# A third nested mixing product in layer two of a two-layer attention and gMLP kernel

## The chip, the cores and the metric

One core of one Trainium2 chip runs one launch of the kernel. TensorE (PE) multiplies, VectorE (DVE) and ScalarE (ACT) do elementwise work, GpSimd (POOL) does a little of that and issues some DMAs, SyncE (SP) issues most DMAs. The metric is the device time in microseconds. Three runs of the kernel before gave 1369.42 (median), 1368.47 and 1369.64.

## The reference

Everything is float32, S = 2048 tokens, D = 512, hidden half width 896. The kernel computes two layers, each an attention block and a mixer block with their own residuals; both layers use the same weights:

```python
def _A_ref(x, wqkv, wo):            # linear attention, 32 heads of 16
    q, k, v = ...                   # x @ wqkv
    phi = lambda t: jnp.where(t > 0, t + 1, jnp.exp(t)) + 1e-6
    kv = einsum("bhsd,bhse->bhde", phi(k), v); z = phi(k) summed over tokens
    ...                             # phi(q) kv / (phi(q) z + 1e-6), heads joined, @ wo

def _B_ref(x, w_in, w_sp, b_sp, w_out):
    z = _gelu(x @ w_in); z1 = z[..., :Fh]; z2 = _layernorm(z[..., Fh:])
    g = einsum("ts,bsf->btf", w_sp, z2) + b_sp[None, :, None]
    return (z1 * g) @ w_out

x = x + _A_ref(_layernorm(x), wqkv, wo)
x = x + _B_ref(_layernorm(x), w_in, w_sp, b_sp, w_out)
x = x + _A_ref(_layernorm(x), wqkv, wo)
x = x + _B_ref(_layernorm(x), w_in, w_sp, b_sp, w_out)
```

## The kernel before

**Number format.** A float32 operand is split into a rounded high part, made by ACT (`high`, L105), and a low part, value minus high, made by DVE (`low`, L108). A product is three matmuls: high by high, high by low, low by high (`mm3`, L119 to L121, and `acc`, L1389 to L1391).

**Stages of a layer.** P1 is the first attention phase over 16 token tiles: project K and Q, form phi, and accumulate the product of the tokens with phi(K). Then a transition, P2 (second attention phase and the mixer's first projection with gelu), a tail, P4 (the token mixing with `w_sp`, 2048 by 2048, then the gates and the output projection, called OUT below). Layer one's OUT also prepares layer two: `Make` (L173) builds kept sums of a weight, and `join` (L1611 on) loads and splits K's and Q's weights and starts the first tiles.

**One step of P1** (`P1.run`). Step s turns token tile s (DVE transpose L296, high L105 on ACT, `T_low` with L108 on DVE), projects K and, up to step 10, Q of tile s - 1 on TensorE, makes phi of each (ACT L363 and L364, DVE L365), splits the normalised tokens (L105, L108) and phi(K) (ACT L376, DVE L377), adds phi(K) to a running sum on POOL (L382), and multiplies tile s - 2 into the accumulators. TensorE's step has 36 matmuls in steps 3 to 10 and 24 in step 2 and from step 11 to step 16, since the last six Q products are put off. `ln_a` (statistics on DVE L230 and L232, three one-column operations on POOL L234, L235, L239) and `ln_b` (normalise on ACT, L245, and a store to be turned) run two steps ahead. From step 5 on pieces of later weights are split at the step's end (`piece`: a high on ACT, a low on DVE), one in step 5, then two until none is left.

**The mixing** (class `P4`). A Strassen-like scheme in seven block products over halves of tokens. P4, P1, P6, P7, P5 and P3 are its products; P1 and P2 of the top level can each be done by seven products of a second level ("nested", N1 and N2, operand halves from halves of token tiles). The order is a tuple of names, one for each layer:

```python
ORDERS = ("P4", "P1", "P6", "P7", "P5", "P3", "N2"), ("P4", "P6", "P7", "N1", "N2", "P5", "P3")
```

P4 and P5 have 8 steps of 24 matmuls, P6, P7 and P3 8 of 18, a nested product 14 of 12. Step g prepares the weight's split of step g + 2 and the token operand of step g + 3 (`prepare`, L1231 on: L1244 and L1253 for the weight, L1228 among the operands' sums, L1257 for their low), multiplies (`mm`, `nested_mm`), fetches the weight of step g + 4. After a product `evac` (L1427, L1448 for P5) or the end of `nested_mm` adds the banks into the gate units. A nested product needs sums of the mixing weight's blocks; class `Inner` makes them (`unit`, `finish`): load, add in place, high, low, two stores to DRAM, 16 kept pairs for each product. Layer two's N1 makes them in P2 and in the mixing's steps `MIX_UNITS`; N2's are left from layer one.

**Gates.** `gates` (L1404 on) multiplies a finished unit by the loaded z1 on POOL (L1411), with a subtraction ahead of it for some (L1409).

**OUT** (second loop of `P4.run`, and `o`). Step i: load the residual two tiles ahead, up to two gates, 21 matmuls of the output projection, the residual's add from the bank (L1514 on DVE), store, then `zsplit(i + 2)`: high of the gates' tile on ACT, low on DVE (L108, 896 columns). In layer one `Make.step` follows (four half sums, L186 to L189, then two highs and lows), and `late_adds` (L1472) at the start.

**What sets the order.** There is no scheduler: each engine runs its instructions in the program's order, and waits on semaphores that a framework places by use of tiles. Tiles come from hand-kept free lists (`pages` of 128x512, `quads`, `banks`), so a tile taken again waits for its last reader.

Of the kernel before, what the change touches and what calls it, by code (L numbers as in the profile page):

```python
# [15 lines left out]
P = 128  # L16
# [13 lines left out]
MIX_UNITS = (11, 15, 18, 20, 25, 31, 36, 40), (7, 9, 11, 13, 15, 17, 19, 21)  # L30
# [3 lines left out]
class Slots:  # L34
# [16 lines left out]
    def put(self, *tiles):  # L51
        for t in tiles:
            n, _ = self.held.pop(id(t))
            self.free_list.append(n)


@with_exitstack
def mixer_kernel(ctx: ExitStack, tc: tile.TileContext, x_in, wqkv, wo_d, win1_d, win2_d, wsp_d, bsp_d, wout_d,
# [114 lines left out]
    class Make:  # L173


        def __init__(self):
            self.raw, self.sum, self.part = {}, {}, {}

        def fetch(self, g):
            self.raw[g] = load(win1_d[g]), load(win1_d[g + 3])  # L180

        def add(self, g):
            a, b = self.raw.pop(g)
            A11, A12, A21, A22 = (r.rearrange("p (c f) -> p c f", f=P)[:, s] for r in (a, b) for s in (slice(0, 2), slice(2, 4)))
            s, t = pages.get([P, 2, 2, P]), pages.get([P, 2, 2, P])
            nc.vector.tensor_add(s[:, 0], A21, A22)  # L186
            nc.vector.tensor_sub(s[:, 1], s[:, 0], A11)
            nc.vector.tensor_sub(t[:, 0], A11, A21)
            nc.vector.tensor_sub(t[:, 1], A12, s[:, 1])  # L189
            pages.put(a, b)  # L190
            self.sum[g] = s, t

        def split(self, g):
            self.part[g] = []
            for r in self.sum.pop(g):
                h, l = pages.get([P, 2, 2, P], F32R), pages.get([P, 2, 2, P], F32R)
                split(h, l, r)
                pages.put(r)
                self.part[g] += [h, l]

        def store(self, g):
            for n, p in enumerate(self.part.pop(g)):
                m = 2 * (n // 2)
                nc.sync.dma_start(kept[:, m:m + 2, g, n % 2, :], p.bitcast(F32).rearrange("p m c f -> p m (c f)"))
                pages.put(p)

        def step(self, i):
            for g in range(3):
                at = i - 2 * g
                if 0 <= at < 5:  # L210
                    (self.fetch, lambda g: None, self.add, self.split, self.store)[at](g)
# [89 lines left out]
    class P1:  # L301
        def __init__(self, L):
# [8 lines left out]
            self.zacc = None  # L311

        def loadx(self, i):
            if i < NT:
                self.x[i] = load(xs[self.st, i])

        def ln_a(self, i):
            if i < NT:
                self.ms[i] = stats(self.x[i], 1, self.L + i == 0)

        def ln_b(self, i):
            if i >= NT:
# [173 lines left out]
        def run(self):  # L496
# [3 lines left out]
            self.wv = quads.get([P, 4, 512])  # L500
            ND = NT - DEFER
            for s in range(1, NT + 2):
                self.loadx(s + 3)
# [19 lines left out]
                if s <= NT:  # L523
                    self.xsplit(s - 1)
                    self.K_split(s - 1)
                if s + 1 < NT and s + 1 in self.turn.by_pe:
# [8 lines left out]
                if s <= 4:  # L535
                    c = s - 1
                    nc.sync.dma_start(self.wv[:, c, :], wqkv[c * P:(c + 1) * P, 1024:1536])
                else:
                    for _ in range(min(len(side), 1 if s < 6 else 2)):
                        side.popleft().piece()  # L540
                if s >= 4:
                    for w in list(side)[:1 if s < 5 else 2]:
# [73 lines left out]
    class P2:  # L616
# [200 lines left out]
        def fetch_sum(self, m):  # L817
            self.S[m] = []
            for g in range(3):
                t = pages.get([P, 2, 2, P], F32R)  # L820
                nc.gpsimd.dma_start(t.rearrange("p i c f -> p i (c f)"), kept[:, m - 1, g])
# [85 lines left out]
        def side(self, s):  # L907
# [7 lines left out]
            elif s == 17:  # L915
# [3 lines left out]
                self.fetch_sum(2)  # L919
            elif s == 18:  # L920
# [3 lines left out]
                self.fetch_sum(3)  # L924

        def run(self, sums):
            w1 = self.win1
            own = inner["N1" if self.seven else "N2"]
            for s in range(1, NT + 3):
# [28 lines left out]
                else:  # L958
# [19 lines left out]
                    if s <= NT + 1:  # L978
                        if not sooner:
                            self.d_high(s - 2)  # L980
                        if 6 <= s < 13 if self.seven else 14 <= s < 18:
# [18 lines left out]
                if self.seven:  # L1000
# [3 lines left out]
                    elif s in (8, 11):  # L1004
                        own.unit()
# [65 lines left out]
    class Inner:  # L1071
# [3 lines left out]
        def __init__(self, base):  # L1075
            self.base = base
            self.d = {m: dram.tile([2, P, 2, 2, 512], F32, name=f"n{base}_{m}") for m in range(1, 5)}
# [4 lines left out]
            self.free = None  # L1082

        def part(self):
            if self.free is None:
                return pages.get(PAGE, F32R)
# [4 lines left out]
        def fetch(self):  # L1091

            if self.ahead:
                k, u = self.ahead.popleft()
                b = self.base
                at = (((3, b), (3, b + 4)), ((2, b),), (), ((2, b + 4),))[u]
                for name, (n, s) in zip(("21", "22") if u == 0 else ("11",) if u == 1 else ("12",), at):
                    self.raw[name] = load(wsp_d[n, s + k])

        def out(self):  # L1100
            for m, k, n, p in self.parts:
                nc.sync.dma_start(self.d[m][k // 2][:, k % 2, n, :], p.bitcast(F32))
                if id(p) in pages.held:
                    pages.put(p)
            self.parts = []

        def finish(self, late=False):
# [7 lines left out]
            if not keep:  # L1115
                pages.put(t)
            self.parts = [(m, k, n, p) for n, p in enumerate((h, l))]
# [31 lines left out]

        def begin(self, n, ahead=2):  # L1150
# [6 lines left out]
    class P4:  # L1157
# [4 lines left out]
        ORDERS = ("P4", "P1", "P6", "P7", "P5", "P3", "N2"), ("P4", "P6", "P7", "N1", "N2", "P5", "P3")  # L1162
# [3 lines left out]
        NEST = ("P1", "P2", "P6", "P5", "P7", "P3", "P4")  # L1166
        OWN = {"P1": (2, 0), "P2": (2, 4), "P4": (3, 4)}
        SUM = {"P3": 4, "P5": 1, "P6": 2, "P7": 3}

        def __init__(self, p2, sums):  # L1170
# [11 lines left out]
            self.wout = {}  # L1182
            self.wraw = deque()
            self.wsteps = (48, 50, 51, 53, 55, 56, 57) if self.nest_late else range(60, 67)
            self.wloads = (45, 47, 48, 50, 52, 53, 54) if self.nest_late else range(60, 67)

        def fetch(self, g):
# [3 lines left out]
            if p[0] == "N" and self.NEST[k // 2] in self.SUM:  # L1191
# [483 lines left out]
```

## Time and profile before

| | |
|---|---|
| median of 3 runs | 1369.42 us (1368.47 to 1369.64) |
| span of the profiled execution | 1367.4 us, 18070 instructions |
| PE / DVE / ACT / POOL busy | 1361.1 / 990.2 / 618.1 / 462.5 us |
| DMA | 287.02 MB, mean 210 GB/s |
| PE stages of layer two, start | OUT of layer one 615.1, P1 691.2, transition 808.2, P2 823.6, tail 1002.9, P4 1026.0, P6 1069.5, P7 1102.2, N1 1134.8, N2 1172.9, P5 1211.0, P3 1254.5, OUT 1287.1 |

The span runs from the profile's first to its last event; the timed runs contain some time around it. A row of a timeline gives an instruction's start and duration, engine and line, output and inputs by tile name, and in brackets how long its engine was idle before and what it waited for. Matmuls overlap, so a matmul's shown duration isn't its share of the time; the distance between starts is. In the page's busy times PEld is the weight load, which lies beside PE.

### The profile page before, as it was taken

The numbers are of one execution on the slowest core, as the hardware profiler recorded it, in microseconds if no ns is written. First come the engines' busy times: TensorE is split into PE (matmuls) and PEld (weight loads), VectorE is DVE, ScalarE is ACT, GpSimd is POOL, SyncE is SP. The second block draws the span as 40 slices with busy tenths as digits, with TensorE's granted clock in tenths as the row PEclk, the third lists the DMA queues.
The fourth block names the chain that finished last, engine by engine and source line by source line (L and its number), as shares of the span: only waits on it lengthen the run. The fifth ranks groups of instructions, "written<-read, shape, count | busy, mean of one in ns | idle before, by whom it ended". The sixth has DMA issues, their size and how long they took to land.

```text
span 1367.4 us, 18070 instructions
## 1 busy us (share of the span) xinstructions
PE 1361.1 (100%) x6129; PEld 1141.0 (83%) x6129; DVE 990.2 (72%) x1471; ACT 618.1 (45%) x978; POOL 462.5 (34%) x537
## 2 busy tenths in 40 slices
PE   9999999999999999999999999999999999999998
PEld 7888888888888888888888888888888888888887
DVE  6775888765757789887667758887767578985742
ACT  6675544444443443441356655534454452442410
POOL 3333475433334137524123434543220001133350
PEclk9999999999999999999999999999999999999999
DMA  5542377877788988897944414777366569854452
GB/s 171 177 131 63 116 246 257 263 247 270 256 249 282 309 277 275 267 355 228 314 124 158 138 56 132 227 224 250 115 198 195 176 225 323 308 183 162 171 189 90
DMA packets 168957, 287.02 MB, mean 210 GB/s; under 512 B 14624, under 2 KB 58528, under 8 KB 165792
## 3 DMA queue, kind: packets, MB, share of 16 engines
q1 hardware_dynamic: 161808, 254.27, 57.7%
q0 software_dynamic: 5184, 28.31, 5.7%
q10 hardware_dynamic: 1872, 3.28, 0.6%
q8 instruction: 48, 0.79, 0.2%
q14 instruction: 45, 0.37, 0.1%
HBM read 196.94 MB, written 88.87 MB: 209 GB/s over the span
## 4 chain that ended last, share of the span: by engine, by line
PE 100%; DVE 0%; DVEq 0%; issue 0%
PE bank L121 19%; PE bank L120 19%; PE bank L119 19%; PE bank L1389 10%; PE bank L1390 10%; PE bank L1391 10%; PE bank L1329 3%; PE bank L1332 3%; PE bank L1331 3%; PE bank L840 1%; PE bank L841 1%; PE bank L839 1%; PE bank L257 1%; PE bank L580 1%; PE bank L445 0%; PE bank L476 0%
## 5 line engine op out<-in xcount | busy, mean ns | idle before, releaser
L1389 PE MATMUL bank<-qd,pg 128*128 128x512 f32 x608 | 236.5, 389 | 0.0
L1390 PE MATMUL bank<-qd,pg 128*128 128x512 f32 x608 | 236.5, 389 | 0.0
L1391 PE MATMUL bank<-qd,pg 128*128 128x512 f32 x608 | 236.5, 389 | 0.0
L1253 DVE TENSOR_TENSOR qd<-qd,qd 128x1024 fp32r<-128x1024 f32 x106 | 145.6, 1373 | 79.0 <-ACT qd L1244 78.4
L1244 ACT ACTIVATE qd<-qd 128x1024 fp32r<-128x1024 f32 x106 | 112.1, 1058 | 128.1 <-DVE qd L1253 52.6
L105 ACT ACTIVATE pg<-pg 128x512 fp32r<-128x512 f32 (+1 forms) x141 | 87.0, 620 | 165.7 <-DVE pg L296 49.4
L121 PE MATMUL bank<-qd,pg 128*128 128x512 f32 x380 | 148.4, 391 | 0.0
L234 POOL TENSOR_SCALAR rs<-mv 128x1 f32<-128x1 f32 x95 | 40.8, 430 | 305.1 <-DVE mv L232 304.7
L1050 POOL TENSOR_TENSOR pg<-pg,pg 128x512 f32<-128x512 f32 x64 | 95.9, 1499 | 135.8 <-DMA pg<-in_wsp_dram 106.4
L1391 PEld LDWEIGHTS bank<-qd,pg 128*128 128x128 f32 x608 | 114.1, 188 | 23.9
L1389 PEld LDWEIGHTS bank<-qd,pg 128*128 128x128 f32 x608 | 114.1, 188 | 23.7
L1390 PEld LDWEIGHTS bank<-qd,pg 128*128 128x128 f32 x608 | 114.1, 188 | 23.5
L1411 POOL TENSOR_TENSOR bg<-bg,pg 128x512 f32<-128x512 f32 x56 | 89.3, 1606 | 127.3 <-DMA pg<-z 123.0
L245 ACT ACTIVATE pg<-pg,nb,rs 128x512 f32<-128x512 f32 x63 | 51.1, 812 | 143.1 <-POOL nb L239 127.6
L119 PE MATMUL bank<-qd,pg 128*128 128x512 f32 x284 | 110.7, 390 | 0.0
L120 PE MATMUL bank<-qd,pg 128*128 128x512 f32 x284 | 110.6, 389 | 0.0
L108 DVE TENSOR_TENSOR pg<-pg,pg 128x512 fp32r<-128x512 f32 (+1 forms) x139 | 102.5, 739 | 11.1 <-DMA z<-pg 3.7
L119 PE MATMUL bank<-bg,qd 128*128 128x448 f32 x256 | 94.0, 367 | 0.0
L120 PE MATMUL bank<-bg,qd 128*128 128x448 f32 x256 | 93.6, 366 | 0.0
L121 PE MATMUL bank<-bg,qd 128*128 128x448 f32 x256 | 93.4, 365 | 0.0
L296 DVE STREAM_TRANSPOSE pg<-pg 128x512 f32<-128x512 f32 x79 | 85.4, 1081 | 9.9 <-DMA pg<-xt 3.4
L119 PE MATMUL bank<-wo,qd 128*128 128x512 f32 x224 | 87.1, 389 | 0.0
(192 smaller groups left out, 3053.9 us busy)
## 6 DMA issues: line engine op xcount, KB each, us to landing
qd<-s SPq DMA_DIRECT2D x64, 512.0 KB, 4.0
pg<-in_wsp_dram SPq DMA_DIRECT2D x96, 256.0 KB, 4.6
qd<-n POOLq DMA_DIRECT2D x24, 1024.0 KB, 7.9
qd<-in_wsp_dram SPq DMA_DIRECT2D x42, 512.0 KB, 4.4
s<-pg SPq DMA_DIRECT2D x64, 256.0 KB, 4.2
pg<-x SPq DMA_DIRECT2D x64, 256.0 KB, 3.6
n<-pg SPq DMA_DIRECT2D x60, 256.0 KB, 4.2
pg<-z SPq DMA_DIRECT2D x56, 256.0 KB, 4.1
```

The source lines that it names most:

```text
L105: nc.scalar.activation(h, src, AF.Copy)
L108: nc.vector.tensor_sub(l, src, h.bitcast(F32))
L119: nc.tensor.matmul(out, ah, bh, start=start, stop=False)
L120: nc.tensor.matmul(out, ah, bl, start=False, stop=False)
L121: nc.tensor.matmul(out, al, bh, start=False, stop=stop)
L1050: nc.gpsimd.tensor_tensor(t, a, b, op=OP.add)
L1244: nc.scalar.activation(wh, r, AF.Copy)
L1253: nc.vector.tensor_sub(wl, r, wh.bitcast(F32))
L1389: m(out, h[:, o], w[:, 0, j, :], start=start, stop=False, skip_group_check=True)
L1390: m(out, h[:, o], w[:, 1, j, :], start=False, stop=False, skip_group_check=True)
L1391: m(out, l[:, o], w[:, 0, j, :], start=False, stop=stop, skip_group_check=True)
L1411: nc.gpsimd.tensor_tensor(u, u, z1, op=OP.mult)
```

## The change

Layer two's product P4 is done as a third nested product, N4, at the end of the mixing.

- The order becomes P6, P7, N1, N2, P5, P3, N4. N4 runs its seven inner products as P1, P6, P2, P5, P7, P4, P3, and adds its banks straight into gate units that are filled by then (two operations each; six units get a copy on ACT during N2, steps 6 to 11). P5's eight steps each get two more DVE operations that prepare N4's operands (`fourth_operand`). P6's operand takes one add more. The gates of layer two move: eight single ones in P5, none in P3, six in N4, fourteen in OUT.
- N4's 16 kept pairs are made by a new method `staged`, one pipeline stage in each step: store the last pair, low of the one before (DVE), high of the one before that (ACT), add of the next (DVE), load ahead. Two adds lie in the last two steps of layer one's OUT, ten in P1's steps 1 to 10 of layer two (their lows up to step 12), four in the mixing's steps 47, 49, 51, 53. In P1 `staged` stands behind `K_split`, ahead of phi(Q), and takes its tiles from two quads cut in pages (`Views`). N1's pairs use `staged` too, in P2's steps from 6 on and the mixing's steps 1, 3, ..., 15.
- Layer two's first normalisation moves from P1 to layer one's OUT: statistics of tile i behind its residual add, `norm(i - 1)` on ACT at step i, a turned store; P1 then loads the normalised tile twice, once as it is and once turned. `ln_a` and `ln_b` do nothing in layer two.
- Pieces of later weights in layer two's P1: one in each of steps 5 to 15. V's weight is loaded in step 15.
- `Make` sums in place, at steps 1, 3 and 5, and splits one half in a step (2 to 7).
- Layer two's output weight is split earlier, in P5, P3 and N4, and OUT takes tokens 8 to 15 first.

Counted by engine, PE's rows go from 6014 to 5990, DVE's from 1440 to 1510, ACT's from 991 to 1017, POOL's from 542 to 544, SP's from 865 to 903.

```diff
-MIX_UNITS = (11, 15, 18, 20, 25, 31, 36, 40), (7, 9, 11, 13, 15, 17, 19, 21)
+MIX_UNITS = (11, 15, 18, 20, 25, 31, 36, 40), (1, 3, 5, 7, 9, 11, 13, 15)
+MAKE_AT = 0, 2, 4
+INNER_UNITS = range(47, 55, 2)
...
@@ P1 @@
+        def norm(self, i):
+            if i < 0:
+                return
+            x, y = self.x.pop(i), pages.get(PAGE)
+            normalise(feats(y, True), feats(x, False), self.ms.pop(i))
+            pages.put(x)
+            self.y = y
...
@@ P1.run @@
             for s in range(1, NT + 2):
+                if s == 2 and own is not None:
+                    self.send(NT - 1)
+                self.loadx(s + 3 if own is None else s + 1)
...
                     self.K_split(s - 1)
+                if own is not None and s <= NT:
+                    own.staged()
+                    if s == 1:
+                        self.norm(NT - 1)
...
@@ Inner @@
+        def staged(self, more=True):
+            self.out()
+            if self.open is not None:
+                m, k, h, t, keep = self.open
+                l = self.part() if keep else t
+                low(l if keep else t.bitcast(F32R), t, h)
...
+            if self.added is not None:
+                m, k, t, keep = self.added
+                h = self.part()
+                high(h if h.dtype == F32R else h.bitcast(F32R), t)
...
+            k, u = self.todo.popleft()
+            op = nc.vector.tensor_tensor
+            if u == 0:
+                self.S1 = t = self.raw.pop("22")
+                op(t, self.raw["21"], t, op=OP.add)
...
-        ORDERS = ("P4", "P1", "P6", "P7", "P5", "P3", "N2"), ("P4", "P6", "P7", "N1", "N2", "P5", "P3")
+        ORDERS = ("P4", "P1", "P6", "P7", "P5", "P3", "N2"), ("P6", "P7", "N1", "N2", "P5", "P3", "N4")
+        NEST["N4"] = "P1", "P6", "P2", "P5", "P7", "P4", "P3"
...
+        def fourth_operand(self, k):
+            a, b = ztile[k], ztile[k + HT]
+            nc.vector.tensor_sub(a[:, self.H1], a[:, self.H2], b[:, self.H1])
+            nc.vector.tensor_sub(a[:, self.H3], b[:, self.H3], a[:, self.H3])
...
@@ P4.nested_mm @@
+            if p == "N4":
+                for n, out in {"P1": ((1, self.X),), "P6": ((2, self.X),), "P2": ((1, self.Y),), "P5": ((4, self.Y),),
+                               "P7": ((4, self.X),), "P3": ((2, self.Y),), "P4": ((3, self.X),)}[name]:
+                    for i in range(2):
+                        f = i if n % 2 else 2 + i
+                        u = self.unit(n // 3, f)
+                        (V.tensor_add if f == 3 else V.tensor_sub)(u, u, out[i])
...
@@ P4.run @@
             for i in range(NT):
                 self.loadx(i + 2)
                 self.gates(2)
+                if nxt is not None:
+                    nxt.norm(i - 1)
+                    if i == NT - 1:
+                        nxt.T(1)
+                self.o(self.order[i], nxt)
+                if nxt is not None:
+                    nxt.ms[i] = stats(nxt.x[i], 1)
+                    nxt.send(i - 1)
                 self.zsplit(i + 2)
+                if nxt is not None:
                     make.step(i)
                     self.join(i, nxt)
```

More of the change, by code (lines that the diff above doesn't have):

```diff
@@ L54, in put, with __init__, get, close @@
             self.free_list.append(n)
+class Views:
+    def __init__(self, pages, *tiles):
+        self.pages = pages
+        self.free_list = deque(t[:, n // 2, n % 2] for n in range(4) for t in tiles)
+        self.held = {}
+    def get(self, shape, dtype=F32):
+        if not self.free_list:
+            return self.pages.get(shape, dtype)
+        t = self.free_list.popleft()
+        self.held[id(t)] = t
+        return t
+    def put(self, t):
+        if id(t) not in self.held:
+            self.pages.put(t)
+            return
+        self.free_list.append(self.held.pop(id(t)))
+    def close(self):
+        assert not self.held
 @with_exitstack
@@ L201, in store @@
-        def store(self, g):
[L202 to L205, printed above, removed]
+            b, a = self.raw[g]
+            A11, A12, A21, A22 = (r[:, s] for r in (a, b) for s in (slice(0, 256), slice(256, 512)))
+            nc.vector.tensor_add(A22, A21, A22)
+            nc.vector.tensor_sub(A21, A11, A21)
+            nc.vector.tensor_sub(A11, A22, A11)
@@ L980, in run @@
                             self.d_high(s - 2)
-                        if 6 <= s < 13 if self.seven else 14 <= s < 18:
+                        if not self.seven and 14 <= s < 18:
                             own.unit()
@@ L1338, in nested_mm @@
             V = nc.vector
+            if p == "N4":
[5 more added lines that the diff above has]
+                        (V.tensor_add if f == 3 else V.tensor_sub)(u, u, out[i])
+                if name in ("P2", "P3"):
+                    banks.put(*self.Y)
+                elif name == "P4":
+                    banks.put(*self.X)
+                if name == "P3":
+                    self.ready.extend((n, f, False) for n in range(2) for f in range(NF))
+                return
             for i in range(2):
@@ L1629, in mixer_kernel @@
     sums = Sums()
[L1630 removed]
+    inner = {"N1": Inner(2, 0, 0), "N2": Inner(2, 8, 8), "N4": Inner(0, 8, 0)}
     p1 = P1(0)
```

280 lines of the change are left out of this document (175 added, 105 removed).

## The prediction

> **What bounds the kernel now.** I read the page's busy times and its chain first, then what the matmul engine waits for.
>
> ```profile
> PE 1361.1 (100%) x6129; PEld 1141.0 (83%) x6129; DVE 990.2 (72%) x1471; ACT 618.1 (45%) x978; POOL 462.5 (34%) x537
> ...
> PE 100%; DVE 0%; DVEq 0%; issue 0%
> ```
>
> ```profile
> PE bank L445 <- DVE pg L440: 2.4, 1, 2.4
> ```
>
> TensorE is busy for 1361.1 of 1367.4 us, is all of the chain, and waits once, 2.4 us at the start. So the time falls with each matmul that goes, and rises with each wait of TensorE that comes; no other engine's work counts until TensorE waits for it. The median of the runs, 1369.42, lies 2.0 us above the span; I work on the profile and lay the differences on the median.
>
> The stages, from the table of windows (PE busy, PEld, DVE, ACT, POOL, each with its count; clock; DMA share; GB/s):
>
> ```profile
> 615.10:691.20 76.10, 76.10 (x337) 63.03 (x336) 53.06 (x71) 21.14 (x30) 20.62 (x21) 1.00 0.75 249
> 691.20:808.20 117.00, 117.00 (x518) 96.86 (x517) 79.94 (x127) 75.63 (x127) 38.62 (x54) 1.00 0.44 133
> ...
> 1026.00:1069.50 43.50, 43.50 (x193) 36.04 (x192) 27.51 (x45) 20.02 (x29) 0.00 (x0) 1.00 0.57 180
> ...
> 1134.80:1172.90 38.10, 38.10 (x170) 31.54 (x169) 34.02 (x64) 12.93 (x24) 4.23 (x8) 1.00 0.89 310
> 1172.90:1211.00 38.10, 38.10 (x170) 31.55 (x169) 33.00 (x55) 14.77 (x26) 5.53 (x9) 1.00 0.86 309
> 1211.00:1254.50 43.50, 43.50 (x194) 36.02 (x193) 33.06 (x31) 15.31 (x23) 18.97 (x11) 1.00 0.41 134
> ```
>
> The first two are layer one's output and layer two's first attention phase, both about 70% full on DVE. The third is layer two's product P4, the next two N1 and N2, the last P5.
>
> **What the change removes.** P4 has 8 steps of 24 matmuls, 192 (its window catches one of a neighbour); N4 has 14 of 12, 168. A 128x512 matmul is shown at 389 ns on the page, but these overlap: the P4 window holds 193 in 43.50 us, 0.225 us each, and N1's 170 in 38.10, 0.224. The windows' edges blur that by one matmul; two of ACT's operations that wait for TensorE, 24 matmuls apart, start 783.96 - 778.52 = 5.44 us apart (rows below). So 24 fewer are worth **5.44 us** (by the 389 ns it would be 9.3, into which the windows' counts don't fit). That is the whole gain: the normalisation, the kept sums and the gates were never on the chain.
>
> **What it adds to the first attention phase of layer two.** This decides, so I follow DVE through one step. First the start of step 2 on DVE, then step 3 from one L296 to the next, then ACT's high and POOL's sum of that step.
>
> ```profile
> 701.48 1.07 DVE L296 STREAM_TRANSPOSE pg<-pg 128x512 f32<-128x512 f32 x1
> ```
>
> ```profile
> 707.65 0.69 DVE L365 SCALAR_TENSOR_TENSOR z_q<-bank,z_q 128x512 f32<-128x512 f32 x1 [1.16 <-ACT z_q L364]
> 708.26 1.07 DVE L296 STREAM_TRANSPOSE pg<-pg 128x512 f32<-128x512 f32 x1
> 709.18 0.64 DVE L230 BATCH_NORM_STATS2 st<-pg 128x6 f32<-128x512 f32 x1
> 709.92 0.18 DVE L232 BATCH_NORM_AGGREGATE mv<-st 128x2 f32<-128x6 f32 x1
> 710.10 0.69 DVE L108 TENSOR_TENSOR pg<-pg,pg 128x512 fp32r<-128x512 f32 x1
> 711.18 0.69 DVE L365 SCALAR_TENSOR_TENSOR pg<-bank,pg 128x512 f32<-128x512 f32 x1 [0.39 <-ACT pg L364]
> 711.79 0.68 DVE L108 TENSOR_TENSOR pg<-pg,pg 128x512 fp32r<-128x512 f32 x1
> 712.57 0.69 DVE L377 SCALAR_TENSOR_TENSOR pg<-pg,pg 128x512 fp32r<-128x512 f32 x1
> 714.42 0.69 DVE L365 SCALAR_TENSOR_TENSOR z_q<-bank,z_q 128x512 f32<-128x512 f32 x1 [1.16 <-ACT z_q L364]
> 715.03 1.07 DVE L296 STREAM_TRANSPOSE pg<-pg 128x512 f32<-128x512 f32 x1
> ```
>
> ```profile
> 709.36 0.63 ACT L105 ACTIVATE pg<-pg 128x512 fp32r<-128x512 f32 x1 [1.75 <-DVE pg L296]
> ```
>
> ```profile
> 713.40 1.29 POOL L382 TENSOR_TENSOR pg<-pg,pg 128x512 f32<-128x512 f32 x1 [1.51 <-DVE pg L377]
> ```
>
> The step is a relay between DVE and ACT, 6.77 us from L296 to L296. The statistics (L230, L232) that leave it lay in the wait for ACT's high (709.36 + 0.63 = 709.99), so their going saves nothing: phi's L365 at +2.92 and L377 at +4.31 stay. Behind L377 the change puts a staged low and a staged add, both with two SBUF inputs; L377 and L108 take 0.60 to 0.61 us from start to start. POOL's sum L382 asks at +5.14, when the staged low has run 0.23 us. What POOL does to DVE then, layer two's P5 and layer one's output show (POOL, then DVE, twice):
>
> ```profile
> 1215.73 2.11 POOL L1411 TENSOR_TENSOR bg<-bg,pg 128x512 f32<-128x512 f32 x1 [24.20 <-DMA pg<-z]
> ```
>
> ```profile
> 1214.20 0.69 DVE L1257 TENSOR_TENSOR pg<-pg,pg 128x512 fp32r<-128x512 f32 x1
> ...
> 1215.46 1.23 DVE L1253 TENSOR_TENSOR qd<-qd,qd 128x1024 fp32r<-128x1024 f32 x1
> 1216.60 1.79 DVE L1257 TENSOR_TENSOR pg<-pg,pg 128x512 fp32r<-128x512 f32 x1
> ```
>
> ```profile
> 650.16 1.29 POOL L1411 TENSOR_TENSOR bg<-bg,pg 128x512 f32<-128x512 f32 x1 [7.14 <-DMA pg<-z]
> ```
>
> ```profile
> 650.19 1.55 DVE L186 TENSOR_TENSOR pg<-pg 128x256 f32<-128x256 f32 x1
> 651.77 0.43 DVE L187 TENSOR_TENSOR pg<-pg,pg 128x256 f32<-128x256 f32 x1
> ```
>
> A POOL operation that asks while L1253 runs lets it end, and the next DVE operation takes 1.79 instead of 0.69: **1.10 us late**. At 650 a sum that POOL shows at 1.29, as L382 is, costs DVE 1.55 - 0.43 = 1.12. DVE operations that read a bank, transposes and statistics show no such delay. In the kernel before, L382 falls into DVE's wait ahead of L365 and costs nothing; in the changed one the staged add stands there.
>
> So the period that DVE and ACT run at by themselves becomes, in steps 2 to 4: 4.31 + 0.60 (L377) + 0.60 (low) + 1.10 (POOL) + 0.60 (add) + 0.61 (L365) = 7.82. From step 5 on a piece of a weight's low comes behind, 0.60 (two take 1.20 here):
>
> ```profile
> 753.91 1.28 DVE L108 TENSOR_TENSOR bg<-pg,bg 128x512 fp32r<-128x512 f32 x2
> 755.12 1.08 DVE L296 STREAM_TRANSPOSE pg<-pg 128x512 f32<-128x512 f32 x1
> ```
>
> Steps 5 to 10: 8.42. Steps 11 and 12 have no add and no second phi, but the staged low and a piece, which now bears the 1.10: 4.31 + 0.60 + 0.60 + 1.10 + 0.60 = 7.21. Steps 13 to 15, with a piece alone: 5.51. TensorE's step is 36 matmuls, 8.16 us, in steps 3 to 10, and 24, 5.44, from step 11; ACT's relus that wait for TensorE show that beat:
>
> ```profile
> 778.52 0.60 ACT L363 ACTIVATE pg<-bank 128x512 f32<-128x512 f32 x1 [0.44 <-PE bank L121]
> ...
> 783.96 0.60 ACT L363 ACTIVATE pg<-bank 128x512 f32<-128x512 f32 x1 [0.32 <-PE bank L121]
> ```
>
> The relu at 778.52 follows the first 12 matmuls (2.72 us) of step 12, which thus begins at 775.75. It multiplies the x that DVE turned in step 11; that low waits for ACT's high, there 1.73 after L296, and takes 0.69; with 0.04 for each signal it is done at 2.50. From 701.48 in step 2 (whose start TensorE and ACT set): 3 x 7.82 + 6 x 8.42 = 73.98 gives 775.46 in step 11, so the low is there at 777.96 and TensorE waits 2.2. Each of steps 13 and 14 then waits 7.21 - 5.44 = 1.77, steps 15 and 16 0.07 each: **5.9 us** in all. Up to step 11 DVE is early enough. Bounds: with a hold of 1.29 the eleven colliding steps are 0.19 longer, 8.0; without collision the periods are 6.72 and 7.32, below 8.16, and the wait is 0.
>
> [...]
>
> **What it adds to layer one's output.** DVE's first operations of three of its steps, then two lows of the weight sums that met gates:
>
> ```profile
> 620.62 1.08 DVE L108 TENSOR_TENSOR qd<-bg,qd 128x896 fp32r<-128x896 f32 x1
> 621.63 0.69 DVE L1472 TENSOR_TENSOR bg<-bg,bank 128x512 f32<-128x512 f32 x1
> 624.78 0.69 DVE L1514 TENSOR_TENSOR pg<-pg,bank 128x512 f32<-128x512 f32 x1 [2.47 <-PE bank L121]
> ...
> 629.54 0.69 DVE L1514 TENSOR_TENSOR pg<-pg,bank 128x512 f32<-128x512 f32 x1 [3.07 <-PE bank L121]
> ```
>
> ```profile
> 636.29 3.48 DVE L108 TENSOR_TENSOR pg<-pg,pg 128x512 fp32r<-128x512 f32 x2
> ```
>
> A step is 629.54 - 624.78 = 4.76 us. The low of the gates (L108, 1.01 to the next) must be there one step after the add L1514 begins; the statistics now come ahead of it: 0.60 + 0.92 + 1.01 = 2.53, slack 2.23. In steps 2 to 6 there are also five weight lows (3.0), eight quarter sums in steps 3 and 5 (some 0.34 each, 2.7) and nine gates: 12.65 + 3.0 + 2.7 + 9.9 if every gate costs 1.10 (636.29 shows two lows at 3.48, 2.2 over 1.28) = 28.3 against 23.8. Less the slack, a wait of **2.3 at most**; 0 if gates fall on adds and statistics, which they do not delay. A step that runs late moves its adds and statistics under the gates, so I take 0.5.
>
> **The rest at about nothing.** N4 uses the same banks in adjacent products, P1 then P6 and P7 then P4: an eviction of 0.69 (L1514's row) must end before the bank is written again, with half a step's matmuls (1.37) between; 0.3, bounds 0 and 2 x 0.69. N4's operands and evictions add to P5, where DVE is busy 33.06 of 43.50; some 5 us of operands and eight gates at 1.10 still fit, less what the evacuation no longer gates; 0 to 1. N1's sums move ahead by some steps, into P6 and P7 and the end of attention; N2's window carries 309 GB/s without a wait of TensorE, so the 9 MB of staged loads and stores on the first attention phase's 133 GB/s (twelve units of three 256 KB transfers, 77 GB/s more) are hidden; SP's queue issues them behind the turned x, and if that cover went, L296 would be late in every step as computed above. POOL loses 13 triples of small operations there.
>
> **Sum:** 1369.42 - 5.44 + 5.9 + 0.5 + 0.3 = **1370.7**. On the profile's span, 1368.7.
>
> **Rivals.** *No collision* (faster): L382 slips in elsewhere, or DVE has more lead. Against it, it asks 0.23 us into the staged low in every step; for it, a few tenths of slack decide steps 11 to 14. 1369.42 - 5.44 + 0.5 = 1364.5, up to 1366.6 with a third of the wait. *Gates in layer one's output* (slower): the zs lows come late by the full 2.3: 1369.42 - 5.44 + 5.9 + 2.3 + 0.3 = 1372.5. It decides from about 2.0 us there, once all waits pass 8.2. *The whole hold* (slower): POOL blocks DVE for 1.29: 1369.42 - 5.44 + 8.0 + 0.5 + 0.3 = 1372.8, slower from a hold of about 1.24 on; against it the 1.10 and 1.12. *N4 gains nothing*: if N4 took P4's 43.5 us because its evictions bind, 1370.7 + 5.4 = 1376.1; against it N1 and N2 at 38.1 with DVE at 34.0 and 33.0.
>
> **Chances.** What this kernel's measurement can tell from no change is about 0.2%, 2.74 us: 1366.7 to 1372.2. The forecast has 0.45, of which 0.05 falls below that band, 0.34 in it and 0.06 above; no collision 0.32, of which 0.30 below; the gates 0.11, the whole hold 0.09, N4 0.03. Faster 0.35, same 0.36, slower 0.29. The range runs from the case without collision less half a microsecond to the whole hold with the gates' 2.3 (1369.42 - 5.44 + 8.0 + 2.3 + 0.3 = 1374.6).
>
> **What would show it.** In the changed profile N4 should fill about 38.2 us. In the first attention phase, the staged add should show 1.7 to 1.8 us instead of 0.69 in steps 2 to 10, L296 should come every 7.8 and 8.4 us, and TensorE should wait on lows of the turned x around 776 to 791 us, some 2.2, 1.8 and 1.8. If the adds show 0.69 there, the collision is refuted, and the time is near 1364.5. TensorE's waits in layer one's output, on the lows of the gates, tell the second term. If TensorE waits on a weight that a DMA brings, or in the mixing, I was wrong in what I costed at nothing.

## The result and the profile after

Eleven runs of the changed kernel gave 1374.07 us in the median (1372.68 to 1379.61), eleven of the kernel before 1369.25 (1368.47 to 1372.48). The ratio is **1.004**, 95% interval 1.0028 to 1.0052: slower by 0.4%, about 5 us, where I had forecast 1370.7 and no difference that can be told. The span of the profiled run is 1372.4 us against 1367.4.

The changed kernel's page, busy times and chain:

```profile
PE 1359.8 (99%) x6105; PEld 1135.9 (83%) x6105; DVE 1024.9 (75%) x1541; ACT 627.2 (46%) x1004; POOL 468.9 (34%) x539
...
PE 23%; DVE 3%; DMA 1%; ACT 1%; issue 1%; POOL 0%; DVEq 0%; ACTq 0%; POOLq 0%
```

TensorE has 24 matmuls less and is busy 1.3 us less, yet the span is longer: it waits now, and some of its matmuls start further apart. What it waits for, longest first:

```profile
PE bank L146 <- ACT z_h L132: 3.2, 2, 2.0
PE bank L1452 <- DVE bg L1468: 2.6, 1, 2.6
PE bank L496 <- DVE pg L491: 2.4, 1, 2.4
```

The first row is layer two's first attention phase (the high of the turned tokens), the second N4 (an eviction), the third the wait at the start, which was there before. The stages that moved, in the table of windows, with layer one's output ahead of them:

```profile
614.80:690.90 76.10, 76.10 (x337) 63.06 (x336) 58.77 (x95) 30.96 (x43) 45.55 (x57) 1.00 0.87 285
690.90:814.50 123.60, 120.40 (x518) 97.14 (x517) 98.31 (x128) 72.91 (x128) 25.08 (x18) 0.99 0.59 180
1009.40:1033.00 23.60, 23.50 (x104) 19.07 (x104) 14.51 (x26) 15.39 (x26) 6.74 (x11) 1.00 0.79 250
1098.30:1136.80 38.50, 38.42 (x170) 31.48 (x169) 36.54 (x68) 15.14 (x27) 4.25 (x8) 1.00 0.90 321
1251.00:1292.30 41.30, 38.62 (x170) 31.38 (x169) 29.64 (x44) 15.72 (x24) 15.42 (x15) 1.00 0.79 293
```

Layer one's output is as long as before. The attention phase is 123.5 us long instead of 117.0 (**+6.5**, by the starts of its matmuls), the tail 23.6 instead of 23.1 and N1 38.5 instead of 38.1 (+0.4 each), and N4 takes 41.3 where P4 took 43.5 (**-2.2**, of the 5.4 that 24 matmuls are worth). Together +5.1. Of the attention phase's 6.5 us, 3.2 are waits in the list; the rest is in the busy time, 120.4 us for the 518 matmuls that took 117.0 before: gaps too short for the list, and matmuls that start further apart.

**The attention phase.** VectorE and GpSimd in step 3:

```profile
709.03 1.07 DVE L327 STREAM_TRANSPOSE pg<-pg 128x512 f32<-128x512 f32 x1
...
713.94 0.68 DVE L135 TENSOR_TENSOR qd<-pg,qd 128x512 f32<-128x512 f32 x1
714.55 1.78 DVE L1244 TENSOR_TENSOR qd<-qd,qd 128x512 f32<-128x512 f32 x1
716.25 0.68 DVE L416 SCALAR_TENSOR_TENSOR z_q<-bank,z_q 128x512 f32<-128x512 f32 x1
716.85 1.07 DVE L327 STREAM_TRANSPOSE pg<-pg 128x512 f32<-128x512 f32 x1
```

```profile
714.25 1.53 POOL L433 TENSOR_TENSOR pg<-pg,pg 128x512 f32<-128x512 f32 x1 [6.29 <-issue]
```

The staged add (L1244) shows 1.78 instead of 0.69; GpSimd asked 0.31 us after the staged low had begun; the turn L327 comes 7.82 us after the last one, the figure that was predicted. TensorE in step 12:

```profile
775.03 0.39 PE L148 MATMUL bank<-pg,pg 128*128 128x512 f32 x1
777.45 0.50 PE L146 MATMUL bank<-qd,z_h 128*128 128x512 f32 x1 [2.04 <-ACT z_h L132]
777.79 0.48 PE L147 MATMUL bank<-qd,z_h 128*128 128x512 f32 x1
778.18 0.80 PE L148 MATMUL bank<-qd,pg 128*128 128x512 f32 x1
778.77 0.63 PE L146 MATMUL bank<-qd,z_h 128*128 128x512 f32 x1
779.20 0.63 PE L147 MATMUL bank<-qd,z_h 128*128 128x512 f32 x1
```

The wait was predicted to end at 777.96 and to be 2.2 long: the low's first reader, L148, starts at 778.18. TensorE starts a little sooner, since the first two matmuls need the high alone. Behind it the matmuls stand 0.43 us apart instead of 0.23, and the window shows a granted clock of 0.59:

```profile
777.40:781.60 4.20, 4.15 (x11) 3.02 (x12) 3.61 (x6) 3.31 (x7) 0.81 (x1) 0.59 0.29 109
```

**N4.** The chain of waits ahead of the long wait at 1281 (start, length, what), then VectorE's row at the weight's low:

```profile
1265.20 10.52 DMA qd<-in_wsp_dram
...
1275.82 1.07 ACT qd L1361
...
1276.91 1.17 DVE qd L1370
...
1279.41 0.53 DVE qd L1370
...
1280.46 0.69 DVE bg L1468
...
1281.29 0.47 PE bank L1452
```

```profile
1276.91 1.23 DVE L1370 TENSOR_TENSOR qd<-qd,qd 128x1024 fp32r<-128x1024 f32 x1 [2.66 <-ACT qd L1361]
```

A raw weight takes 10.5 us to land (4.4 in the median of the kernel before). VectorE, in order, waits 2.66 us for its high, does its low, three smaller lows and the next weight's low, and only then the eviction L1468 of P7's banks (adding them into the gate units), which P4's first matmul needs. From 1265 to 1282 us 390 GB/s are moved at a DMA share of 1.04. Full DMA engines alone don't make TensorE wait, though: N2 in the kernel before moves more for as long without a wait:

```profile
1182.00:1199.00 17.00, 17.00 (x77) 14.08 (x76) 13.37 (x27) 3.94 (x9) 2.94 (x5) 1.00 1.06 417
```

There eight kept sums stand in a row, land in 5.1 to 8.2 us and are used as they are; the next two raw weights are asked for when most of them are in, and land in 6.4 and 5.2 us. A raw weight is split two steps (5.4 us) ahead of its use, so it is wanted that much earlier than a kept sum asked for in the same step, and those of N4's P4 came among kept sums and took 10.5 and 9.5 us. That this is what tells N4 from N2 is read from the program and these times; no experiment tests it.

### The profile page after: what moved, and what is told of

The parts are those of the page before. It is cut to its first block, busy times and chain, and to the rows that moved or that the text cites. A ratio compares the mean times of both kernels' runs of the same rounds, so it can differ in the third digit from the quotient of the medians.

```text
span 1372.4 us, 18248 instructions
## 1 busy us (share of the span) xinstructions
PE 1359.8 (99%) x6105; PEld 1135.9 (83%) x6105; DVE 1024.9 (75%) x1541; ACT 627.2 (46%) x1004; POOL 468.9 (34%) x539
## 5 line engine op out<-in xcount | busy, mean ns | idle before, releaser
L1526 PE MATMUL bank<-qd,pg 128*128 128x512 f32 x544 | 211.6, 389 | 0.0
L1527 PE MATMUL bank<-qd,pg 128*128 128x512 f32 x544 | 211.6, 389 | 0.0
L1528 PE MATMUL bank<-qd,pg 128*128 128x512 f32 x544 | 211.6, 389 | 0.0
L132 ACT ACTIVATE pg<-pg 128x512 fp32r<-128x512 f32 (+1 forms) x154 | 94.9, 620 | 152.8 <-DVE pg L327 60.8
L148 PE MATMUL bank<-qd,pg 128*128 128x512 f32 x380 | 149.7, 394 | 0.2 <-DVE pg L135 0.2
L1117 POOL TENSOR_TENSOR pg<-pg,pg 128x512 f32<-128x512 f32 x64 | 92.7, 1449 | 138.6 <-DMA pg<-in_wsp_dram 84.4
L265 POOL TENSOR_SCALAR rs<-mv 128x1 f32<-128x1 f32 x95 | 46.9, 493 | 262.6 <-DVE mv L263 253.7
L135 DVE TENSOR_TENSOR pg<-pg,pg 128x512 fp32r<-128x512 f32 (+1 forms) x151 | 110.5, 733 | 18.7 <-ACT pg L132 11.2
L1527 PEld LDWEIGHTS bank<-qd,pg 128*128 128x128 f32 x544 | 102.1, 188 | 21.4
L1526 PEld LDWEIGHTS bank<-qd,pg 128*128 128x128 f32 x544 | 102.1, 188 | 21.2
L1528 PEld LDWEIGHTS bank<-qd,pg 128*128 128x128 f32 x544 | 102.1, 188 | 21.0
L146 PE MATMUL bank<-qd,pg 128*128 128x512 f32 x284 | 110.6, 390 | 0.0
L147 PE MATMUL bank<-qd,pg 128*128 128x512 f32 x284 | 110.6, 389 | 0.0
L327 DVE STREAM_TRANSPOSE pg<-pg 128x512 f32<-128x512 f32 x79 | 85.4, 1081 | 13.2 <-DMA z<-pg 4.9
L148 PE MATMUL bank<-bg,qd 128*128 128x448 f32 x256 | 93.5, 365 | 0.0
L1452 PE MATMUL bank<-qd,pg 128*128 128x512 f32 x224 | 87.3, 390 | 2.7 <-DVE bg L1468 2.6
```

The costliest lines, as they stand in the source:

```text
L132: nc.scalar.activation(h, src, AF.Copy)
L135: nc.vector.tensor_sub(l, src, h.bitcast(F32))
L146: nc.tensor.matmul(out, ah, bh, start=start, stop=False)
L147: nc.tensor.matmul(out, ah, bl, start=False, stop=False)
L148: nc.tensor.matmul(out, al, bh, start=False, stop=stop)
L1117: nc.gpsimd.tensor_tensor(t, a, b, op=OP.add)
```

## The experiments

Two theories at first. Mine: the collision of GpSimd's sum with the staged operations makes the attention phase long, and late weights make N4 long. Its rivals: VectorE simply has too much work in a step; and N4's evictions bind by themselves, or the transfers' total does.

**1. The staged operations at another place of the step.** From the changed kernel; `early_low`, `early_add` and `late_high` are the parts of `staged`.

```diff
                 if turned:
                     self.T_high(s)
+                if own is not None and s <= NT:
+                    own.early_low()
...
                 if turned:
                     self.T_low(s)
+                if own is not None and s <= NT:
+                    own.early_add()
...
                 if own is not None and s <= NT:
-                    own.staged()
+                    own.late_high()
```

> The changed kernel with the same operations in layer two's first attention phase, two of them at another place of the step on VectorE: the staged low stands right behind the turn of the tokens (where VectorE waits for ScalarE's high), the staged add behind the low of the turned tokens (where it waits for phi's exponential); the staged high stays. GpSimd's running sum then meets operations that read a bank, or none. Theory (the collision with GpSimd's sum is what makes the steps 7.85 to 8.5 us long): the staged adds show 0.69 instead of 1.78, the steps are 8.2 and 5.45 long as TensorE sets them, TensorE doesn't wait there, the phase is 117.1 us instead of 123.6, and the time is about 1374.1 - 6.5 = 1367.6, 0.12% under the kernel before. Rival (VectorE has too much work in the step, whatever its order): the steps stay as long, 1373 to 1374.

Measured: 1367.5 us (1365.81 to 1370.44), ratio to before 0.9988 (0.9979 to 0.9998). VectorE and GpSimd in step 3:

```profile
707.38 1.08 DVE L327 STREAM_TRANSPOSE pg<-pg 128x512 f32<-128x512 f32 x1
708.31 0.67 DVE L135 TENSOR_TENSOR qd<-pg,qd 128x512 f32<-128x512 f32 x1
709.16 0.69 DVE L135 TENSOR_TENSOR pg<-pg,pg 128x512 fp32r<-128x512 f32 x1 [0.18 <-ACT pg L132]
709.77 0.69 DVE L1284 TENSOR_TENSOR qd<-qd,qd 128x512 f32<-128x512 f32 x1
...
713.45 0.69 DVE L416 SCALAR_TENSOR_TENSOR z_q<-bank,z_q 128x512 f32<-128x512 f32 x1 [0.98 <-ACT z_q L415]
714.05 1.07 DVE L327 STREAM_TRANSPOSE pg<-pg 128x512 f32<-128x512 f32 x1
```

```profile
712.60 1.29 POOL L433 TENSOR_TENSOR pg<-pg,pg 128x512 f32<-128x512 f32 x1 [5.38 <-DMA pg<-xt]
```

The add L1284 shows 0.69, GpSimd's sum 1.29, as alone, in VectorE's wait before L416; VectorE's period is 6.67 us, under TensorE's 8.16, and the phase takes 116.97. The same operations on the same engines cost 6.5 us in one place and nothing in the other. That is the theory, and the rival of too much work is out.

**2. The running sum on VectorE.**

```diff
-                nc.gpsimd.tensor_tensor(r, self.zacc, r, op=OP.add)
+                (nc.gpsimd if self.L == 0 else nc.vector).tensor_tensor(r, self.zacc, r, op=OP.add)
```

> The changed kernel with layer two's running sum of phi(K) moved from GpSimd to VectorE, the staged operations where they are: 0.60 us more work for VectorE in each step, and nothing for it to collide with. Theory (collision, 1.10 a step): the steps become 7.35 (2 to 4), 7.95 (5 to 10), 6.7 (11, 12) and 6.1 (13 to 15) long for VectorE; TensorE waits only at the end, about 1.5 us in steps 13 to 16 together, with no low clock behind it: 1369 to 1369.5. Rival (too much work on VectorE): 0.60 a step is added to what is too long, the phase is longer than 123.6 us and the time over 1375.

Measured: 1370.73 us, ratio 1.0017 (1.0008 to 1.0027); the phase is 120.3 long. More work on VectorE made the kernel 3.3 us faster, so the direction is the theory's; the size is not quite. TensorE's waits on the turned tokens:

```profile
PE bank L146 <- ACT z_h L132: 1.1, 3, 0.8
```

The long gaps are 0.92, 0.35 and 0.33 us, the 1.5 that I expected, but the phase lost 3.3. Behind each such start the next three matmuls come 0.11, 0.16 and 0.11 us too late again (the second of them is the first to read the low, which VectorE makes behind the high), some 0.4 a step in four steps: a step that VectorE paces costs a little more than its wait.

**3. N4's raw weights earlier.**

```diff
-                self.fetch(g + 4)
+                if self.nest_late or g not in (66, 67):
+                    self.fetch(g + 4)
+                if not self.nest_late and g in (65, 66):
+                    self.fetch(g + 5)
```

> The changed kernel with the two raw weights of N4's sixth inner product (P4) fetched one step earlier, ahead of the load of another step; the first attention phase is untouched. Theory (TensorE's 2.7 us wait at 1281 is these weights' late landing, which holds up VectorE's queue with the eviction in it): N4 takes 38.3 to 38.7 us instead of 41.3, the time is about 1371.3. Rival one (the evictions between two products on the same banks bind by themselves): the wait stays, 1374. Rival two (the transfers' total is the limit, 390 GB/s there): the loads only share what there is, land under 1 us earlier, and another weight is late instead: 1373 to 1374.

Measured: 1373.52 us, ratio 1.0033 (1.0022 to 1.0044); N4 takes 40.4 us in its profile. The edit hardly moved the loads: counted from N4's start, the first weight was asked for at 13.8 us instead of 14.2 and the second at 16.5 as before, since the tile that it lands in was still being read. The first landed 3.0 us earlier (7.97 us after its issue instead of 10.52), the second 0.2 later, and TensorE waited on a kept sum, and less on the eviction:

```profile
PE bank L1452 <- DMA qd<-n: 1.3, 1, 1.3
PE bank L1452 <- DVE bg L1468: 0.5, 1, 0.5
```

That is what the rival of the transfers' load said, a wait that moves to another weight. With both edits together,

> Both edits together: staged low and add early in the step, N4's two raw weights one step earlier. If the two waits are all that stands between the change and its gain of 5.4 us: about 1369.3 - 5.4 + 0.8 for the small waits left (in the tail and N1) = 1364.6, 0.34% under the kernel before. If clearing one wait uncovers another of its size: 1366 or more.

1366.96 us came out, ratio 0.9985 (0.9977 to 0.9994): clearing the first wait leaves N4's, as the last sentence had it; N4 takes 40.4 us here too.

**4. Less to load in N4.** From here on all kernels have the edit of experiment 1. In N4's first 13 steps the gates' z1 isn't loaded, and the unit is multiplied by itself.

```diff
-                self.z1[n, f] = load(z1s[self.L, n, f])
+                self.z1[n, f] = None if self.inside_n4 else load(z1s[self.L, n, f])
...
-                nc.gpsimd.tensor_tensor(u, u, z1, op=OP.mult)
+                nc.gpsimd.tensor_tensor(u, u, u if z1 is None else z1, op=OP.mult)
```

> The kernel with the staged low and add early in the step, and without the six 256 KB loads of z1 that belong to N4's gates: those six units are multiplied by themselves instead (part of the computation is left out), so that GpSimd's operations stay. Theory (the sum of the transfers sets when N4's weights land; four 1 MB sums in a row with z1 among them ask for some 390 to 400 GB/s): with 1.5 MB less the weights land 3 us earlier, N4 takes 38.1 to 38.5 us instead of 39.8 to 41.3, the time is 1364.5 to 1365.5, and the runs spread less than the 1365.8 to 1370.4 of the kernel with those loads. Rival (the order of the queues, not their load, holds the weights; or the evictions): no change, 1367.5.

Measured: 1365.38 us (1364.67 to 1366.61), ratio 0.9973 (0.9963 to 0.9983), as forecast; N4 takes 39.2 us in its profile, longer than forecast. The kernel of experiment 1 left one profile, of the fastest of its ten runs (1365.81, where the median is 1367.5), with N4 at 39.8, so the profiles show less of the difference than the medians. The middle of N4 in the kernel of experiment 1, and here:

```profile
1255.00:1272.00 17.00, 15.99 (x72) 12.92 (x71) 16.19 (x23) 7.83 (x15) 6.25 (x8) 1.00 1.05 400
```

```profile
1255.00:1272.00 17.00, 16.87 (x75) 13.64 (x73) 16.87 (x24) 7.90 (x15) 5.93 (x7) 1.00 0.92 338
```

At a DMA share of 1.05 and 400 GB/s the DMA engines are full; at 0.92 what is left of TensorE's waits is 0.9 us at an eviction. The kept sums that GpSimd's queue asks for from 1250 to 1258 us, in the kernel of experiment 1 and here (count, size, median time to landing):

```profile
qd<-n POOLq DMA_DIRECT2D x3, 1024.0 KB, 7.4
```

```profile
qd<-n POOLq DMA_DIRECT2D x3, 1024.0 KB, 5.2
```

The first two are asked for at the same time after N4's start in both, 6.1 and 8.6 us, in a queue that has no z1 load, and land 2.2 and 3.1 us sooner: the load is what makes the kept sums late. P4's two raw weights, asked for 0.4 us earlier and at the same time, land only 0.4 and 0.6 us earlier, and the 0.9 us go back to the second of them (8.55 us to land). One difference besides the load is left: GpSimd's gate reads one tile instead of two and shows 1.05 us instead of 1.3 to 1.7.

**5. The peaks spread.** N4's inner products in another order, P2 on banks of its own.

```diff
-        NEST["N4"] = "P1", "P6", "P2", "P5", "P7", "P4", "P3"
+        NEST["N4"] = "P5", "P1", "P6", "P2", "P7", "P4", "P3"
```

> The kernel with the staged low and add early in the step, and N4's inner products in the order P5, P1, P6, P2, P7, P4, P3, so that the products whose weights are kept sums (1 MB a step) and those whose weights are raw (512 KB a step) alternate; P2 gets banks of its own, the operands' sums are made three steps earlier. All bytes stay. Theory (peaks of the transfers): the weights land in time, N4 takes 38.1 to 38.6 us, the time is 1364.5 to 1365.5, 0.3% under the kernel before. Rival (the total, not the peak): N4's mean stays near 300 GB/s with the other loads, and the wait only moves: 1366.5 to 1367.5.

Measured: 1367.64 us, ratio 0.9994 (0.9985 to 1.0003), and N4 41.7 us long in its profile: the theory's forecast is a miss. Its waits are listed on evictions:

```profile
PE bank L1501 <- DVE bg L1518: 3.0, 2, 2.1
```

The longer one (2.1) goes back to a raw weight all the same, by the path of the changed kernel:

```profile
1262.46 6.86 DMA qd<-in_wsp_dram
...
1269.40 1.06 ACT qd L1408
...
1272.99 0.53 DVE qd L1417
...
1274.05 0.69 DVE bg L1518
```

The weight took 6.9 us to land, less than the 7.6 and 9.1 of P4's raw weights in experiment 1, but was asked for 18.3 us after N4's start, not 14.2, since it waited for a tile that VectorE frees. So this order doesn't tell peak from total. The eviction behind the weight led to the next pair.

**6. The eviction ahead of the weight, and z1 ahead of N4.** The first moves one step's preparation behind its products:

```diff
-                self.prepare(g + 2, g + 3)
+                late = not self.nest_late and g == 69
+                if not late:
+                    self.prepare(g + 2, g + 3)
...
                 self.mm(g)
+                if late:
+                    self.prepare(g + 2, g + 3)
```

> The kernel with the staged low and add early in the step, and in N4's step 69 (the last of P7) the products and the two evictions ahead of the preparation of the weight of step 71 instead of behind it; loads, bytes and queues of the transfers as they were. Theory (the late weight costs so much because VectorE, in order, waits for it with the eviction of P7's banks behind it, and P4 can't start on these banks): the wait between P7 and P4 goes, N4 keeps at most the waits on kept sums that land late, some 1 us; 1366.0 to 1366.8 instead of 1367.5. Rival (the late weight itself is what P4 waits for): no change, 1367.5.

Measured: 1365.89 us, ratio 0.9978 (0.9968 to 0.9989), and what is left in N4 is the wait on a kept sum:

```profile
PE bank L1499 <- DMA qd<-n: 1.8, 1, 1.8
```

The second loads four of N4's six z1 in P3:

```diff
+                if not self.nest_late and p == "P3" and 0 <= k - 4 < 4:
+                    u = divmod(k - 4, 3)
+                    self.z1[2 + u[0], 4 + u[1]] = load(z1s[1, 2 + u[0], 4 + u[1]])
```

> The kernel with the staged low and add early in the step, and four of the six z1 loads of N4's gates done in P3's last four steps, where 215 to 230 GB/s were moved. Theory (the load in N4's middle decides, 1.5 MB less gave 1365.4): 1.0 MB less there gives about two thirds of these 2.1 us, 1366.0 to 1366.5. Rival (the total of P3's end and N4 decides, since kept sums are fetched there already): 1367 to 1367.6.

Measured: 1366.57 us (1366.18 to 1368.73), ratio 0.9982 (0.9973 to 0.9991). Its middle moves 354 GB/s, and the wait that is left is the eviction's, behind a raw weight that took 8.8 us to land:

```profile
1255.00:1272.00 17.00, 17.00 (x77) 14.08 (x76) 16.83 (x23) 7.57 (x14) 6.90 (x8) 1.00 0.97 354
```

```profile
PE bank L1499 <- DVE bg L1515: 1.2, 1, 1.2
```

By the waits that are left there were two links, the load and the queue in front of the eviction, and each edit left the other. What each is worth alone is not shown: N4 takes 40.2 and 40.0 us in the two profiles, 39.8 in that of experiment 1's fastest run, and the runs of the three kernels overlap. All three edits:

> All three edits: staged low and add early, four z1 loads in P3, P7's eviction ahead of the next weight's preparation. If the waits in N4 come from the loads and the queue in front of the eviction, N4 takes 38.2 to 38.6 us and the time is 1364.5 to 1365.3, 0.3% under the kernel before.

Measured: **1364.98 us** (1364.09 to 1367.32), ratio **0.997** (0.9959 to 0.9981), 0.3% faster than the kernel before. N4 is 38.5 us long, the attention phase 117.0. This beats both kernels. The only wait left in N4 that is in the list:

```profile
PE bank L1499 <- ACT qd L1408: 0.2, 1, 0.2
```

**7. One lone wait.** The kernel before with idle work on VectorE in one step.

```diff
                 if turned:
+                    if self.L == 1 and s == 11:
+                        d = pages.get([P, 4, P])
+                        for _ in range(7):
+                            nc.vector.tensor_tensor(d, self.part[0], self.part[0], op=OP.add)
+                        pages.put(d)
                     self.T_low(s)
```

> The kernel before with seven idle adds of 0.60 us on VectorE (4.2 us) ahead of the low of the turned tokens in step 11 of layer two's first attention phase, which before had about 1.8 us of slack, and nothing else: one lone wait of TensorE of about 2.2 to 2.4 us. Theory (a wait costs itself and some 0.4 us of slow restart): 1368.9 + 2.7 = 1371.6, granted clock 1.00 behind it in most runs. Rival (a wait of this length lets the granted clock fall to a half for some 4 us, as once in the changed kernel's profile at 777 us): 2 us more, 1373.6.

Measured: 1372.7 us (1371.36 to 1375.08), ratio 1.0027 (1.0017 to 1.0036). The profiled run shows one wait and no low clock, and its span is 1370.0, 2.6 over that of before:

```profile
PE bank L121 <- DVE pg L108: 2.5, 1, 2.5
```

```profile
778.00:782.00 4.00, 3.44 (x15) 2.83 (x16) 3.89 (x6) 1.79 (x3) 1.30 (x1) 1.00 0.14 41
```

The phase takes 120.1 us instead of 117.0, 3.1 more by a wait of 2.5, so here too a wait costs more than itself. The median is 3.6 over that of before. It lies between the two forecasts; runs with and without a low clock would give that, but the other runs have no trace, and their mean granted clocks, 0.998 to 1.000, don't decide it (the profiled run has 0.999). So this is left open.

## Why the prediction was wrong

- **The gain** was right: 24 matmuls less are worth 5.4 us. With N4's long waits gone (all three edits), it takes 38.5 against P4's 43.5, and 0.24 of that is a small wait left.
- **The attention phase** was right in mechanism, place and nearly in size: +5.9 predicted, +6.5 measured. The periods 7.82 and 8.42 were met (716.85 - 709.03 = 7.82; from step 10 to step 11 it is 8.44), and so was the hold of 1.10: the staged add shows 1.78 us instead of 0.69, 1.09 more, beside a sum of GpSimd that shows 1.53 there and 1.29 when alone. No run shows a hold of the whole 1.29, which the rival's 8.0 us took; the rival of the whole hold is refuted. Which operations are not late was as predicted: begun while GpSimd worked, an add from a bank shows 0.69 us in the changed kernel's trace (L1656 at 629.25), a turn 1.09 (L327 at 158.30; 1.07 at 709.03) and a statistic 0.69 (L261 at 625.22). The remaining 0.6 I have not taken apart; the slow start behind each wait is in it.
- **Layer one's output**: 0.5 predicted, 0 measured; 76.10 of 76.10 us are busy.
- **The step that failed** is "the rest at about nothing": N4 at 0.3, where 3.2 us were lost (41.3 against the 38.1 of N1 and N2 before), 2.6 of them in the one wait at 1281. I weighed only its evictions, by the distance of half a step between two writes of a bank, and took "N2's window carries 309 GB/s without a wait" as cover for transfers elsewhere. I never added up N4's own transfers: kept sums of 1 MB in 8 steps, raw weights of 512 KB in 6, and beside these what N2 has not: z1, the output weight and the residual. N2's window was no cover: it is full in its middle, too (417 GB/s), but with kept sums, and N4's raw weights fell into the full stretch (390 GB/s). They came late, and behind them in VectorE's queue the eviction; N4 falls to 38.5 when load and queue are both relieved. My rule for the eviction was also wrong in form: the eviction started when VectorE came to it (1280.46), not when the bank was done (P7's last matmul starts at 1278.34), and a late weight's low stood ahead of it.
- **The tail and N1**, costed at nothing too, lost 0.4 each. The tail's part was there in some profiles (23.6) and not in others (23.1); N1's in all. I have not followed either.
- Sum, on the spans: -5.4 + 6.5 + 3.2 + 0.4 + 0.4 = +5.1, against 1372.4 - 1367.4 = 5.0. The forecast had -5.4 + 5.9 + 0.5 + 0.3 = +1.3. The time lies inside the range, at its upper end, but on the side of "slower", which had 0.29; and it lies there by a mechanism that none of the rivals named. The nearest, *N4 gains nothing*, had the evictions bind by themselves, which gives 43.5 for N4. What came true is the last of the signs named, a wait of TensorE in the mixing.
- The spread of the changed kernel's runs (1372.7 to 1379.6, where the kernel before has 1368.5 to 1372.5) has no profile behind its upper part. With less load in N4 it was smaller (1364.7 to 1366.6 without z1, 1366.2 to 1368.7 with z1 ahead), which fits N4; the runs of 1378 and more stay unexplained.

## What to carry to other kernels

When an operation with two SBUF inputs is added on VectorE, look what GpSimd does at that moment: the same operation cost 1.10 us more a step in one place and nothing where VectorE was waiting for ScalarE anyway. When a product is replaced by one with fewer multiplications and prepared operands, add up its bytes in its own stage, with all that is loaded there besides and how soon each load is wanted, and not by a stage that merely looks alike. VectorE takes its operations in the program's order, and here an eviction stood behind a weight's low that waited 2.66 us: put the eviction first.

## What the runs showed of the hardware

A wait of about 2 us (2.04 by the row at 777.45) was followed once by a granted clock of 0.59 over 4.2 us, with matmuls 0.43 us apart. In the kernel of experiment 3 the same wait at the same place kept a clock of 1.00, and the phase was as long (123.54 against 123.53), because VectorE set the pace behind it either way (there TensorE waited 1.2 us again at 785, in the changed kernel not): the low clock cost nothing there.

Waits of 2.5 and 2.6 us (experiment 7; N4 in the changed kernel) were not followed by a low clock, so the wait's length alone doesn't decide. In the changed kernel's trace the records of the granted clock begin at 6.54 us, and it changes at 777.96, 781.37 and 1371.87: 771.41, 3.41 and 590.51 us apart, 226, 1 and 173 times 3.4133. In that of the kernel before they begin at 8.48, and it changes at 1366.99, 398 times 3.4133 later. The low spell fills one such stretch. Taken by such stretches (the first number behind the length is TensorE's busy time), the changed kernel ahead of the low spell and in it, then the two stretches that share the wait of experiment 7:

```profile
774.54:777.96 3.42, 1.38 (x6) 0.67 (x4) 2.73 (x5) 1.16 (x3) 0.00 (x0) 1.00 0.80 210
777.96:781.37 3.41, 3.41 (x9) 2.54 (x9) 2.85 (x6) 2.78 (x5) 0.58 (x1) 0.50 0.24 93
```

```profile
774.49:777.91 3.42, 1.53 (x7) 0.94 (x5) 3.28 (x6) 0.18 (x1) 0.54 (x2) 1.00 0.00 0
777.91:781.32 3.41, 2.76 (x12) 2.27 (x13) 3.31 (x5) 1.34 (x2) 0.68 (x1) 1.00 0.00 0
```

The stretch with 2.04 us idle was followed by a clock of 0.50, the one with 1.89 by 1.00. N4's wait falls on two stretches, with 0.99 and 1.57 us idle, and the clock stayed at 1.00; how that of experiment 3 falls on them isn't shown. At the end of the program a stretch with 3.26 us idle (changed kernel) and one with 3.41 (kernel before) were followed by 0.50 and 0.51. So in these few cases a clock of 1.00 followed up to 1.89 us idle in a stretch, and one of 0.50 from 2.04 us on; no experiment varies it.
